# A recurrent attention layer and a two-layer block in one kernel: another written order, constants made on VectorE, and transposes of five late units given to the DMA crossbar

## The chip, the cores and the metric

The kernel runs on one core of one Trainium2 chip. The metric is the device time of one execution in microseconds (us); below it is better. The core has five engines with instruction queues of their own: TensorE (PE in the profile, its weight loads PEld), VectorE (DVE), ScalarE (ACT), GpSimd (POOL) and SyncE (SP), which here only issues DMAs. Every queue is in order: an instruction that waits holds up all behind it on its engine.

## The reference

First a recurrence with a decaying state runs over 768 time steps, for 4 batches and 8 heads of size 48. Its result is reshaped to 3072 tokens of 384 numbers, which pass through a block with a hidden layer of 1024, a softmax-like gate, a normalization and an output product.

```
# r, k, v, w: (4, 8, 768, 48), u: (8, 48)
for t in range(S):
    cur = outer(u * k[t], v[t])
    y[t] = r[t] @ (state + cur)
    state = w[t][:, None] * state + outer(k[t], v[t])
x = y as (3072, 384)
h = x @ w_in                                  # (3072, 1024)
solu = h * softmax(h)
ln = (solu - mean(solu)) / sqrt(var(solu) + 1e-6) * g_ln
out = ln @ w_out                              # (3072, 384), float32
```

## The kernel before

The work is cut into 24 units: six chunks of 128 time steps for each of four batches, chunk by chunk, batch by batch. Unit i works on batch i % 4 and chunk i // 4. So units i and i + 4 are tied by the state of their batch, and units 0 to 3 have no state before them.

A unit goes through these stages; the short names are the words of the written order. Loads: LW, LK, LR, LV bring w, k, r and v of the unit, 192 KB each in rows of 192 bytes. `lw` takes the logarithm of w on ScalarE, `cum` sums it over time with two matmuls against the triangular constants `uti_neg` and `uts`, `ex` takes the exponential in PSUM, and `kp` (DVE) multiplies it with k and r. `krk` and `krr` turn the two halves of the product on TensorE, four 128x128 blocks each, and `kr` copies the result from PSUM into `kr_s`. `M` multiplies the turned k with the turned r, head by head; `m` copies the scores, either with the triangular mask (DVE) or without it (ScalarE), in which case GpSimd masks them afterwards (`sel`). `p`, `q`, `dg` and `dv` make the bonus term with u; `vb` casts v to bf16. `Y` forms y from scores and state, `y` copies it. `S`, `et` and `st` carry the state on. `X` turns y on TensorE in three blocks, and `xT` copies them.

The second part: `H` is the hidden product (24 matmuls), `e` its exponential (ScalarE), `he` the gated value (DVE), `hq` its square. `Oa` and `Ob` are the output product in two halves of the hidden size; beside each output matmul of 385 columns stand two of one column, which sum for the normalization. `sq`, `qm` and `lv` make the scale per token, `o` scales, `out` stores.

One-time work: LI and LO load w_in and w_out (1.5 MB each), `wi` casts, `gw` multiplies w_out with the gain, `mn` takes a column mean with eight matmuls, `mc` copies it, `ce` subtracts it. LU, `us`, `uc` spread u; LG, `gs`, `gc` turn the gain. `hot` is a number of matmuls on zeros, of no use for the result.

Nothing schedules at run time. The order of all stages is written out as one text, `ORDER`, and every word is one call: a stage name, a unit number and, after a dot, an engine (a, d, p), a DMA queue (s for SP, a for ACT) or a PSUM slot. A wrapper, `InOrder`, keeps each engine's instructions in the order in which the calls were made. Because nearly all instructions are recorded inside that wrapper, the profile shows one line for them, L89, and they are told apart by the names of their tiles.

Rings of buffers bound how far one engine runs ahead: 7 for the loads of w, k, r and v, 10 for lw and vb, 6 for kp, kr and dv, 4 for most others. DMAs of SP and ACT share eight completion semaphores in turn, so a DMA also waits until the one eight places earlier has landed. All stores are issued by SP in this kernel.

Before the first word of the order, the constants are made: `warm`, the columns of ones and the zero paddings of `lw` and `kp` by memsets on DVE; the triangles, the identities, `halves`, `off_blocks` and `keep` by memsets and selects on GpSimd. The functions `turned_kr` (KD) and `turned_x` (XD) exist, but no word calls them:

```
    def turned_kr(i, x):
        sp.dma_start_transpose(out=kr_s[i % NKP], in_=kp_t[i % NKP].rearrange("t j h d -> t (j h d)"))

    def turned_x(i, x):
        sp.dma_start_transpose(out=xT_t[i % NWK], in_=y_t[i % NWK])
```

Of the kernel before, what the change touches and what calls it, by code (L numbers as in the profile page):

```python
# [8 lines left out]
F32 = mybir.dt.float32  # L9
BF16 = mybir.dt.bfloat16  # L10
# [11 lines left out]
LW0.a LK0.s LU0.a LR0.s LW1.a LW2.s hot4.s3 LG0.s LK1.s lw0 LV0.a cum0.b0 LR1.s us0.s0 ex0 hot2.s3 uc0 lw1 LV1.s  # L22
p0 kp0 LW3.a LK2.a LR2.s krk0.s3 q0 krr0 cum1.b1 kr0.a hot2.s2 LV2.s LK3.a M0.b0 LR3.s p1 gs0.s1 ex1 m0.d
hot3.s3 LI1.s lw2 q1 dg0 cum2.b0 lw3 hot2.s3 kp1 vb0.p LI0.a S0.s2 dv0 vb1.a dg1 hot1.s3 ex2 Y0.is0 et0 LV3.a
cum3.b1 LI2.s p2 kp2 krk1.s3 gc0 LO0.s ex3 st0 LW4.s krk2.s1 q2 krr1 LO1.s krr2 kp3 kr1.a hot3.s2 dv1 LK4.s
kr2.d y0.a p3 M1.b0 LK5.a S1.s2 dg2 krk3.s3 vb2.a m1.d krr3 et1 wi0.a S2.s0 wi1.p M2.b1 st1 X0.s1 kr3.a m2.d
Y1.is2 LR4.s wi2.p et2 y1.a M3.b0 xT0.d LV4.a X1.s3 q3 m3.d H0.b1 dv2 gw1.a dg3 gw2.d e0 Y2.is2 LW5.s xT1.d
gw3.p st2 H1.b0 y2.a he0 lw4 gw0.a X2.s1 LR5.s e1 gw7.d cum4.b1 gw4.d hot2.s3 gw6.d gw5.d ex4 he1 vb3.p mn0.s3
LW6.s LV5.a dv3 xT2.a LK6.s kp4 S3.s0 mc0 Y3.is2 LR6.s lw5 ce6.d krk4.s1 ce3.d hq0.a cum5.b0 ce4.d krr4 ce2.d
H2.b1 ce7.d ex5 LW7.s ce1.d ce5.d ce0.d y3.a LK7.s p4 kp5 et3 Oa0.s3 lw6 e2 LR7.s kr4.d p5 krk5.s2 cum6.b0 st3  # L30
hq1.a Ob0 vb4.p he2 LW8.s q4 krr5 ex6 S4.s1 LK8.s kr5.d sq0 M4.b1 lw7 Oa1.s0 kp6 et4 m4.a LR8.s X3.s2 qm0 st4
vb5.p M5.b0 xT3.a cum7.b1 dg4 sel4 lv0 krk6.s1 LV6.s Ob1 m5.d ex7 LW9.s dv4 lw8 S5.s2 kp7 o0.a krr6 LK9.s p6
cum8.b0 sq1 et5 Y4.ns3 kr6.d ex8 H3.b1 q5 LV7.s y4.d hq2.a kp8 q6 LR9.s krk7.s1 e3 X4.s3 st5 LW10.s vb6.p M6.b0
krr7 xT4.d Oa2.s2 dg5 m6.a LK10.s qm1 kr7.d dv5 krk8.s3 lv1 Ob2 he3 out0 sel6 o1.a lw9 M7.b0 out1 dg6 S6.s1 sq2
m7.a LV8.s hq3.d krr8 cum9.b1 LR10.s Y5.ns0 vb7.p qm2 kr8.d lv2 H4.b0 p7 LW11.s et6 y5.d ex9 st6 p8 lw10 kp9
LV9.s X5.s3 S7.s0 e4 Oa3.s1 q7 o2.d vb8.a he4 out2 cum10.b1 dv6 xT5.a krk9.s2 et7 LK11.s ex10 Y6.ns3 q8 krr9 st7
LV10.s H5.b0 hq4.a kp10 sel7 LR11.s kr9.a y6.d M8.b1 dg7 LW12.s S8.s0 lw11 m8.d Ob3 dv7 et8 e5 LV11.s vb9.p
krk10.s3 st8 X6.s2 LK12.s p9 M9.b1 he5 xT6.a Y7.ns0 sq3 m9.a krr10 LR12.s S9.s2 dg8 cum11.b0 et9 LW13.s y7.d
H6.b1 lw12 dv8 ex11 kr10.d LK13.s p10 qm3 lv3 kp11 Oa4.s0 LR13.s e6 q9 st9 X7.s3 cum12.b0 LW14.s xT7.a Ob4 he6
p11 ex12 LV12.s krk11.s2 sel9 sq4 Y8.ns3 o3.a kp12 H7.b1 hq5.a out3 vb10.p qm4 y8.d q10 LK14.s lv4 dg9 M10.b0 e7  # L40
Oa5.s1 LR14.s m10.d vb11.p q11 o4.a krr11 LW15.s X8.s3 lw13 dg10 Ob5 p12 xT8.a out4 he7 kr11.a S10.s0 dv9 S11.s3
LV13.s dg11 sq5 hq6.a Y9.ns2 vb12.p qm5 cum13.b0 y9.d dv10 LK15.s H8.b1 et10 ex13 st10 LR15.s et11 lw14 kp13
Oa6.s2 LW16.s e8 hq7.d krk12.s0 lw15 M11.b0 p13 st11 LK16.s Ob6 lv5 he8 o5.a q12 krr12 m11.a Y10.ns3 out5 kr12.d
krk13.s1 cum14.b1 LR16.s y10.d sq6 krr13 sel11 ex14 cum15.b0 LW17.s kr13.d Oa7.s0 ex15 qm6 LV14.s kp14 p14
Y11.ns3 lw16 X9.s1 Ob7 kp15 lv6 dv11 LK17.s vb13.a xT9.d p15 o6.a M12.b1 y11.d M13.b0 m12.a X10.s1 out6 m13.d
krk14.s2 q13 S12.s3 LR17.s hq8.a krr14 H9.b1 dg12 LV15.s vb14.p xT10.d sq7 q14 et12 qm7 st12 LW18.s lv7 krk15.s1
dg13 e9 X11.s3 sel12 H10.b0 o7.d kr14.a out7 he9 dv12 LK18.s Y12.ns0 xT11.a p16 krr15 LR18.s Oa8.s2 e10 y12.d
kr15.d q15 LV16.s cum16.b1 he10 S13.s0 ex16 dv13 Ob8 LV17.s et13 kp16 q16 X12.s3 LW19.s Y13.ns1 sq8 xT12.a st13
M14.b0 vb15.p M15.b1 LK19.s m14.a y13.d krk16.s3 S14.s0 hq9.d krr16 LR19.s m15.a S15.s1 p17 qm8 kr16.d H11.b0
LW20.s et14 dg14 lv8 sel14 st14 et15 LK20.s dg15 H12.b1 e11 vb16.p o8.d sel15 st15 out8 lw17 Oa9.s3 he11 LV18.s  # L50
e12 vb17.p dv14 S16.s0 LV19.s hq10.a he12 Ob9 dv15 LR20.s et16 cum17.b0 st16 q17 Y14.ns2 LV20.s ex17 X13.s1
y14.d M16.b1 sq9 Oa10.s0 lw18 kp17 LW21.s m16.a Y15.ns2 qm9 xT13.d LK21.s cum18.b0 hq11.d lv9 krk17.s1 lw19
H13.b1 LR21.s o9.d p18 vb18.a dg16 ex18 LV21.s y15.d dv16 krr17 e13 Ob10 kp18 LW22.s sel16 X14.s3 hq12.a kr17.d
S17.s2 LK22.s cum19.b0 q18 he13 Oa11.s1 xT14.a LR22.s ex19 p19 X15.s3 lw20 M17.b1 out9 xT15.d Ob11 sq10 kp19
vb20.p m17.a LW23.s q19 Y16.ns3 qm10 dg17 et17 vb19.a cum20.b0 p20 LV22.s y16.d lv10 H14.b1 dg18 sq11 ex20 sel17
LK23.s st17 lw21 o10.d LR23.s Oa12.s3 e14 kp20 dv17 krk18.s2 Ob12 out10 hq13.a p21 qm11 he14 krk19.s0 LV23.s
lv11 krr18 q20 cum21.b0 sq12 o11.d krr19 ex21 H15.b1 p22 qm12 kr18.d out11 lv12 kr19.d vb21.p Oa13.s1 dv18 kp21
e15 X16.s2 o12.d Y17.ns0 xT16.a M18.b0 hq14.a y17.d out12 krk20.s3 Ob13 he15 lw22 X17.s0 m18.a krk21.s2 xT17.d
krr20 cum22.b1 dg19 krr21 sq13 sel18 ex22 qm13 S18.s0 dg20 H16.b0 kr20.d hq15.a q21 kr21.d lv13 kp22 Oa14.s3
dv19 e16 dv20 M19.b1 et18 Y18.ns2 he16 m19.a Ob14 lw23 sel19 y18.d M20.b1 sq14 M21.b0 o13.d Oa15.s2 m21.a st18  # L60
out13 m20.d krk22.s1 X18.s0 cum23.b0 xT18.a krr22 Ob15 ex23 hq16.d vb22.p dg21 kr22.a Y19.ns0 q22 kp23 H17.b1
vb23.a dv21 qm14 sq15 y19.d lv14 Y20.ns1 e17 p23 o14.d H18.b0 dg22 out14 sel21 qm15 y20.d lv15 krk23.s0 he17 e18
Oa16.s3 dv22 krr23 o15.a he18 q23 Ob16 kr23.a out15 X19.s1 M22.b1 xT19.d M23.b0 hq17.d X20.s2 S19.s0 xT20.a
hq18.d Oa17.s1 m22.a dg23 Y21.ns2 et19 m23.a sel22 st19 H19.b1 sq16 sel23 qm16 y21.d lv16 Oa18.s0 e19 dv23
X21.s2 Ob17 he19 H20.b0 sq17 o16.d xT21.d out16 Y22.ns3 qm17 e20 Y23.ns2 y22.d Ob18 y23.d hq19.a he20 H21.b1
lv17 o17.d X22.s3 Oa19.s2 e21 out17 xT22.d hq20.d X23.s1 sq18 H22.b0 he21 xT23.d Ob19 qm18 hq21.d e22 H23.b1
sq19 lv18 qm19 he22 Oa20.s3 e23 o18.d hq22.d Oa21.s1 out18 lv19 he23 Ob20 o19.d Ob21 sq20 hq23.d out19 Oa22.s0
sq21 qm20 qm21 lv20 Oa23.s2 lv21 o20.d o21.d out20 Ob22 out21 Ob23 sq22 qm22 lv22 sq23 qm23 o22.d lv23 out22
o23.a out23
# [27 lines left out]
def kernel(  # L97
# [14 lines left out]
    C = 128  # L112
# [20 lines left out]
    def bank(shape, dtype, slot, name):  # L133
# [15 lines left out]
    dve.memset(warm, 0.0)  # L149
    uti_neg = consts.tile([C, C], BF16)  # L150
    pool.memset(uti_neg, -1.0)
    pool.affine_select(out=uti_neg, in_=uti_neg, compare_op=ALU.is_ge, fill=0.0, base=0,
                       pattern=[[1, C]], channel_multiplier=-1)
    uts = consts.tile([C, C], BF16)
    pool.memset(uts, 1.0)
    pool.affine_select(out=uts, in_=uts, compare_op=ALU.is_gt, fill=0.0, base=0,
                       pattern=[[1, C]], channel_multiplier=-1)
    ident_f = consts.tile([C, C], F32)
    pool.memset(ident_f, 0.0)
    pool.affine_select(out=ident_f, in_=ident_f, compare_op=ALU.not_equal, fill=1.0, base=0,  # L160
                       pattern=[[-1, C]], channel_multiplier=1)
    ident = consts.tile([C, C], BF16)
    pool.tensor_copy(out=ident, in_=ident_f)

    halves = consts.tile([C, C], BF16)
    pool.memset(halves, 0.0)
    pool.memset(halves[0:2, :], 1.0)
    pool.affine_select(out=halves[0:2, :], in_=halves[0:2, :], compare_op=ALU.is_ge, fill=0.0, base=0,
                       pattern=[[1, C]], channel_multiplier=-64)
    pool.affine_select(out=halves[0:2, :], in_=halves[0:2, :], compare_op=ALU.is_gt, fill=0.0, base=64,  # L170
                       pattern=[[-1, C]], channel_multiplier=64)
    off_blocks = consts.tile([C, HP, 2], BF16)
    pool.memset(off_blocks, 0.0)
    pool.memset(off_blocks[0:2], -30000.0)
    pool.affine_select(out=off_blocks[0:2], in_=off_blocks[0:2], compare_op=ALU.not_equal, fill=0.0, base=0,
                       pattern=[[0, HP], [-1, 2]], channel_multiplier=1)

    one_col = consts.tile([C, 2], BF16)
    dve.memset(one_col, 1.0)
    inv_col = consts.tile([C, 1], BF16)  # L180
    dve.memset(inv_col, 1.0 / RDF)
    ones_row = consts.tile([1, C], F32)
    dve.memset(ones_row, 1.0)

    lw_t = ring("lw", NLW, [C, H, 64], BF16)
    kp_t = ring("kp", NKP, [C, 2, H, 64], BF16)
# [369 lines left out]
```

The softmax here doesn't subtract the row's maximum and nothing guards it: scores larger than these inputs give would overflow.

## Time and profile before

| what | us |
|---|---|
| median of 5 runs | 154.59 |
| lowest and highest run | 152.16 and 155.85 |
| profiled execution, its own time | 154.59 |
| span of that execution in the profile | 152.8 |
| PE busy | 137.3 |
| DVE busy | 127.8 |
| ACT busy | 117.8 |
| POOL busy | 95.3 |

The span runs from the first to the last instruction; the time of an execution also holds what lies around it. Busy time of PE is modelled with pipelined matmuls, so it tells that TensorE had work, not that it ran at its peak; the pace is better read from the distance of the starts. The page cuts the span into 40 slices and gives each engine one digit for each, in tenths. The chain goes back from the last instruction, at each step to what released it or to the instruction before it on its engine. A line with SPq or ACTq is a DMA issue on that queue, and its length is the time of the issue.

### The profile page before, as it was taken

What the parts mean: (1) busy time and instruction counts of PE and PEld (TensorE: products, weight loads), DVE (VectorE), ACT (ScalarE), POOL (GpSimd) and SP (SyncE); (2) the same over time, 40 slices, a digit from 0 to 9 for tenths busy, and PEclk for the clock granted to TensorE, in tenths of its full rate; (3) what the DMA queues carried; (4) which work ended last, traced back from release to release, by engine and by line L of the source; (5) the groups of instructions that cost most, each with busy time, mean ns of one, the idle gap of its engine ahead of it and who ended that gap; (6) DMA issues with size and microseconds to landing.
All of it is one profiled execution on the core that took longest, in us unless ns stands there. A gap on an engine that the chain in (4) does not pass through costs nothing.

```text
span 152.8 us, 5260 instructions
## 1 busy us (share of the span) xinstructions
PE 137.3 (90%) x2158; PEld 106.8 (70%) x2158; DVE 127.8 (84%) x235; ACT 117.8 (77%) x238; POOL 95.3 (62%) x127
## 2 busy tenths in 40 slices
PE   4799786879999998999993999999999999999980
PEld 1145565467788876887793797878887888889750
DVE  5209797989999997999983999999998998688941
ACT  3464857499999997999895588999898998475442
POOL 7484993621979769992928999299937691500000
PEclk9999999999999999999999999999999999999999
DMA  5999999899994999989999999999930111011142
GB/s 107 259 259 334 399 328 267 174 205 188 226 197 124 232 186 205 202 196 206 236 203 205 192 191 222 186 212 220 229 114 4 51 56 51 4 51 56 51 158 103
DMA packets 104825, 27.08 MB, mean 177 GB/s; under 512 B 100313, under 2 KB 104418, under 8 KB 104802
## 3 DMA queue, kind: packets, MB, share of 16 engines
q1 hardware_dynamic: 94256, 24.26, 69.4%
q10 hardware_dynamic: 10546, 2.49, 7.2%
q8 instruction: 17, 0.28, 0.7%
q14 instruction: 6, 0.05, 0.1%
HBM read 22.03 MB, written 4.72 MB: 175 GB/s over the span
## 4 chain that ended last, share of the span: by engine, by line
PE 48%; DMA 12%; SPq 11%; DVE 10%; POOL 9%; issue 4%; ACT 3%; ACTq 0%; DVEq 0%; POOLq 0%
PE o_ps L89 21%; PE h_ps L89 12%; SPq L89 11%; DMA w_in<-in_w_dram 8%; DMA kr_in<-in_r_dram 3%; PE kr_ps L89 3%; PE y_ps L89 3%; PE cum_ps L89 3%; POOL p L89 3%; POOL q L89 2%; PE m_ps L89 2%; PE s_ps L89 2%; POOL m L89 2%; DVE kp L89 2%; DVE st L89 2%
## 5 line engine op out<-in xcount | busy, mean ns | idle before, releaser
L89 PE MATMUL o_ps<-w,he 128*128 128x385 bf16 x192 | 45.8, 325 | 0.1
L89 PE MATMUL h_ps<-xT,win_sb 128*128 128x128 bf16 x576 | 35.9, 219 | 0.3 <-DVE xT L89 0.3
L89 PEld LDWEIGHTS <-win_sb 128*128 128x128 bf16 x576 | 33.0, 98 | 0.9 <-issue 0.4
L89 PE MATMUL o_ps<-inv_col,e 128*128 128x1 bf16 x192 | 31.8, 166 | 0.0
L89 PE MATMUL o_ps<-one_col,hq 128*128 128x1 bf16 x192 | 31.4, 164 | 0.0
L89 DVE TENSOR_TENSOR he<-h_ps,e 128x1024 bf16<-128x1024 f32 x24 | 29.1, 1216 | 2.6 <-ACT e L89 2.5
L89 ACT ACTIVATE e<-h_ps 128x1024 bf16<-128x1024 f32 x24 | 24.5, 1020 | 4.7 <-PE h_ps L89 4.6
L89 DVE TENSOR_TENSOR kp<-cum_ps,kr_in 128x768 bf16<-128x768 f32 x24 | 22.7, 949 | 5.7 <-ACT cum_ps L89 5.5
L89 PEld LDWEIGHTS <-hq 128*128 128x128 bf16 x192 | 18.5, 96 | 12.7
L89 POOL TENSOR_TENSOR p<-kr_in 128x384 bf16<-128x384 f32 x24 | 24.7, 1029 | 3.5 <-DMA kr_in<-in_r_dram 3.5
L89 POOL TENSOR_TENSOR dv<-vb,dg 128x384 bf16<-128x384 bf16 x24 | 19.8, 829 | 9.4 <-DVE dg L89 7.3
L89 POOL TENSOR_SCALAR_AFFINE_SELECT m<-m 128x1024 bf16<-128x1024 bf16 x15 | 16.8, 1121 | 12.7 <-ACT sq L89 5.6
L89 POOL TENSOR_TENSOR q<-p,u_bc 128x384 bf16<-128x384 bf16 x24 | 21.8, 910 | 1.9 <-DMA kr_in<-in_k_dram 1.7
L89 ACT ACTIVATE cum_ps<-cum_ps 128x768 f32<-128x768 f32 x24 | 19.2, 802 | 4.7 <-PE cum_ps L89 4.6
L89 PEld LDWEIGHTS <-kp 128*128 128x128 bf16 x272 | 17.5, 98 | 5.8 <-DVE kp L89 2.1
L89 PE MATMUL kr_ps<-ident,kp 128*128 128x128 bf16 x192 | 18.0, 223 | 2.2 <-ACT xT L89 0.9
L89 PEld LDWEIGHTS <-he 128*128 128x128 bf16 x192 | 18.4, 96 | 0.9
L89 PEld LDWEIGHTS <-e 128*128 128x128 bf16 x192 | 18.5, 96 | 0.3
L89 ACT CAST m<-m_ps 128x1024 bf16<-128x1024 f32 x15 | 15.1, 1016 | 0.7 <-PE m_ps L89 0.6
L89 ACT ACTIVATE lw<-w_in 128x384 bf16<-128x384 f32 x24 | 12.4, 523 | 3.7 <-DMA w_in<-in_w_dram 3.7
L89 DVE TENSOR_TENSOR m<-m_ps,keep 128x1024 bf16<-128x1024 f32 x9 | 10.9, 1215 | 4.2 <-PE m_ps L89 4.2
L89 ACT ACTIVATE hq<-he 128x1024 bf16<-128x1024 bf16 x13 | 13.8, 1058 | 0.0
(82 smaller groups left out, 263.0 us busy)
## 6 DMA issues: line engine op xcount, KB each, us to landing
kr_in<-in_r_dram SPq DMA_DIRECT2D x24, 192.0 KB, 4.0
out_dram<-o SPq DMA_DIRECT2D x24, 192.0 KB, 2.9
kr_in<-in_k_dram SPq DMA_DIRECT2D x21, 192.0 KB, 3.7
w_in<-in_w_dram SPq DMA_DIRECT2D x21, 192.0 KB, 3.9
v_in<-in_v_dram SPq DMA_DIRECT2D x20, 192.0 KB, 4.0
wout_f<-in_moe_w_out_dram SPq DMA_DIRECT2D x2, 768.0 KB, 7.7
win_f<-in_moe_w_in_dram SPq DMA_DIRECT2D x2, 512.0 KB, 5.0
v_in<-in_v_dram ACTq DMA_DIRECT2D x4, 192.0 KB, 4.5
```

The lines of the kernel that those rows point to most:

```text
L89: made = make(*args, **kwargs)
```

## The change

The order text is replaced by another. In it:

- `turned_kr` (KD) takes the place of `krk`, `krr` and `kr` for units 19 to 23, and `turned_x` (XD) the place of `X` and `xT` for the same units. Both are DMA transposes on SP's queue, from SBUF to SBUF.
- Eight stores (units 5, 6, 11, 13, 17, 18, 22, 23) and the load of the gain are issued by GpSimd instead of SP. ScalarE issues 9 DMAs instead of 12.
- The bonus is added by DVE in the copy of y for all units but one (20 units before), so one identity matmul in `Y` instead of four.
- `m` with the mask on DVE 12 times instead of 9, `sel` 12 instead of 15; `o` on ScalarE 17 times instead of 8; `hq` on ScalarE 15 instead of 13; two of eight `ce` on GpSimd; 25 warm-up matmuls instead of 19.
- The loads of a unit stand later in the text against the matmuls in the last third; the loads of units 0 to 4, but v of unit 4, stand ahead of w_in and w_out.

Outside the order: the constants become a stage (`pc`) that the order calls; their memsets are on DVE, four selects stay on GpSimd. `halves` and `off_blocks` use rows 0 and 32 instead of 0 and 1 and need no select. `keep` is the same tile as `uts`. u is rounded to bf16 (`ur`) before the matmul that spreads it. Stages that treat a unit in halves are added (hidden, exponential, gate, square, output columns, sums, store); no word of the new order calls them, and the last unit goes through the same stages as the others.

The diff, cut to its core:

```
-LW0.a LK0.s LU0.a LR0.s LW1.a LW2.s hot4.s3 LG0.s LK1.s lw0 LV0.a cum0.b0 LR1.s us0.s0 ex0 hot2.s3 uc0 lw1 LV1.s
...
-sq21 qm20 qm21 lv20 Oa23.s2 lv21 o20.d o21.d out20 Ob22 out21 Ob23 sq22 qm22 lv22 sq23 qm23 o22.d lv23 out22
-o23.a out23
+LG0.p pc0 LW0.s LR0.a LK0.s LR1.a hot6.s3 LU0.s LW1.s LW2.s LV0.s lw0 cum0.b0 LW3.s ur0 hot1.s3 ex0 us0.s0
...
+ex1 krr0 hot6.s2 uc0 LK2.a LW4.s lw2 p1 kp1 kr0.a cum2.b0
...
+Y3.ns3 H1.b1 gw3.d e0 st3 y3.d gw0.a LW6.s gw6.d X3.s0 gw7.d gw4.a gw5.d LK6.s e1 he0 mn0.s2 LR6.s vb4.p lw5 he1
+dv4 xT3.a cum5.b0 mc0 LW7.s S4.s1 ex5 Y4.ns3 ce5.d ce2.d H2.b1 hq0.a ce0.p kp5 vb5.a ce7.d H3.b0 LK7.s ce3.d et4
...
+sq10 ex20 Y16.ns3 out9 qm10 xT15.d H14.b1 sq11 lv10 kp20 KD19 vb19.a o10.a y16.d S16.s1 e14 hq13.d H15.b0 out10
...
+ex23 sel20 qm14 st18 sq15 lv14 kp23 q22 Y19.ns1 o14.a Y20.ns3 y19.d e17 KD23 H18.b0 p23 y20.d he17 q23 Oa16.s0
+out14 e18 XD19 dv21 qm15 S19.s1 lv15 he18 Ob16 hq17.a LV23.s M22.b1 XD20 dg22 o15.a M23.b0 Oa17.s3 m22.d sq16
...
+out16 he19 XD22 Oa18.s0 e20 st19 H21.b1 hq19.a qm17 dg23 he20 dv23 Y23.ns2 e21 Ob18 y23.d lv17 XD23 Oa19.s1 he21
...
+Ob22 o21.a Ob23 out21 sq22 qm22 lv22 sq23 qm23 o22.d lv23 o23.a out22.p out23.p

-    pool.memset(uti_neg, -1.0)
-    pool.affine_select(out=uti_neg, ...)
...
+    keep = uts
+
+    def constants(i, x):
+        dve.memset(warm, 0.0)
+        dve.memset(uti_neg, -1.0)
+        dve.memset(uts, 1.0)
+        dve.memset(ident, 0.0)
+        dve.memset(ident_f, 0.0)
+        pool.affine_select(out=uti_neg, ...)
+        pool.affine_select(out=uts, ...)
+        pool.affine_select(out=ident, ...)
+        pool.affine_select(out=ident_f, ...)
+        ...
+        for row, own in ((0, 0), (32, 1)):
+            dve.memset(halves[row:row + 1, 64 * own:64 * own + 64], 1.0)
+            dve.memset(off_blocks[row:row + 1, :, 1 - own], -30000.0)
...
-    ones_row = consts.tile([1, C], F32)
+    ones_row = consts.tile([1, C], BF16)
...
-    queue = {"s": sp, "a": act}
+    queue = {"s": sp, "a": act, "p": pool}
...
+    def round_u(i, x):
+        dve.tensor_copy(out=u_b, in_=u_row)
...
-    pe.matmul(ps["u"], lhsT=ones_row, rhs=u_row, start=True, stop=True)
+    pe.matmul(ps["u"], lhsT=ones_row, rhs=u_b, start=True, stop=True)
...
-        sp.dma_start(out=out[b * S + c * C:b * S + (c + 1) * C, :], in_=o_t[i % NWK])
+        queue[x or "s"].dma_start(out=out[b * S + c * C:b * S + (c + 1) * C, cols], in_=o_t[i % NWK][:, cols])
```

## The prediction

> **What bounds the kernel now.** I read the page first: the 40 slices, then the chain.
>
> ```profile
> span 152.8 us, 5260 instructions
> PE   4799786879999998999993999999999999999980
> DMA  5999999899994999989999999999930111011142
> GB/s 107 259 259 334 399 328 267 174 205 188 226 197 124 232 186 205 202 196 206 236 203 205 192 191 222 186 212 220 229 114 4 51 56 51 4 51 56 51 158 103
> PE 48%; DMA 12%; SPq 11%; DVE 10%; POOL 9%; issue 4%; ACT 3%; ACTq 0%; DVEq 0%; POOLq 0%
> ```
>
> A slice is 3.82 us. TensorE has holes in the first eight slices and is full afterwards; the DMA engines are full up to slice 30 (some 112 us) and nearly empty later. So the start hangs on transfers and the short queues, the rest on TensorE, with the loads close behind it. The chain in order of time shows where that changes:
>
> ```profile
> 26.11 3.90 DMA w_in<-in_w_dram
> 30.02 0.44 ACTq L89
> 30.50 0.13 ACT xT L89
> ...
> 30.88 0.48 ACT mean_sb L89
> 31.36 0.43 ACT lw L89
> 31.84 0.49 PE cum_ps L89 x2
> ...
> 32.55 1.34 PE h_ps L89 x24
> 33.89 0.87 PE o_ps L89 x12
> ...
> 38.16 0.19 PE x_ps L89 x3
> ...
> 53.85 4.16 DMA w_in<-in_w_dram
> ...
> 141.58 5.98 PE o_ps L89 x84
> ```
>
> The columns are start, length, what. From 31.84 us (cum5 in the written order) the chain is mostly TensorE. Its pieces, these and further ones of the same list, price a stage by its pace: H 1.34, Oa and Ob 0.83 each, krk and krr (four transposes) 0.235 each, X 0.18, cum 0.33, M 0.33, Y 0.38, S 0.46 us. Summed along the written order, 122.1 us of useful TensorE work stand in the whole kernel and 110.1 us from cum5 on. The last matmul ends at 148.40. The busy times by stretch give the holes after 32 us:
>
> ```profile
> 80.00:90.00 10.00, 7.66 (x145) 6.39 (x143) 7.22 (x11) 6.21 (x13) 9.12 (x11) 1.00 0.97 200
> 130.00:140.00 10.00, 10.00 (x176) 8.70 (x174) 8.32 (x16) 5.76 (x13) 2.10 (x3) 1.00 0.12 43
> ```
>
> (stretch, length, busy PE, PEld, DVE, ACT, POOL, clock, DMA share, GB/s). All stretches together leave 3.64 us of holes, 2.34 of them in 80 to 90. So 148.40 - 31.84 - 3.64 = 112.9 us for 110.1 us of prices: one priced us is 1.026 real ones. After the last matmul stand 4.4 us of scaling and store. The profiled execution took 154.59 us, 1.79 beyond its span, and is the median of the five runs (152.16 to 155.85); I sum against it.
>
> **What the Trainium skill says.** "VectorE: DVE Perf Modes", The three transpose paths: a 128x128 bf16 block takes TensorE 390 ns and the DMA crossbar 1309 ns. This trace has TensorE's at 223 ns, pipelined to 59 ns (0.235/4); it has no crossbar transfer. "DMA: Bandwidth & Descriptors", Latency and other measured facts: crossbar transposes move 261 GB/s. Same page, Issuing engines are not separate DMA queues: all queues share the 16 engines; so the new ones queue behind loads. Same page, SWDGE vs HWDGE vs iDMA: descriptors of a GpSimd DMA are written by software; first byte about 1 us against 0.6. The trace has no such DMA.
>
> **The change part by part.**
>
> *TensorE work.* Units 19 to 23 lose krk, krr (2 x 0.235 each) and X (0.18): 5 x 0.65 = 3.25 us. Only one unit instead of four adds its bonus by an identity matmul (0.16 us apart by the starts of the matmuls around it): 0.48. Together 3.73 priced, 3.8 us real, all on a full engine. The six additional warm-up matmuls lie in the first waits. The stages for a unit in halves are defined, but no word of the order calls them: nothing.
>
> *The start.* Constants leave GpSimd (its selects and memsets end at 4.82 us), but lw0 also ends at 4.82, so that alone gives nothing. The u matmul in bf16 takes some 0.3 instead of 1.64 us; krk0 stood behind it and two warm-ups until 8.36. What sets the start is ScalarE. It issued 12 loads and stood behind their semaphores: 2.4 us before gw, 2.1 before xT, 1.4 before gr, 1.3 before vb in the table of waits. Now it issues nine. From lw0 (4.30) to mc0 the new order gives it 6 lw at 0.52, 5 ex at 0.80, 5 kr at 1.01, 4 et at 0.18, 4 xT at 0.48, 2 e at 1.02, 2 vb at 0.51, 3 gw at 0.62, uc, gc, wi0, y2 and mc0 (2.66 together) and seven issues at 0.38: 25.1 us. With the first two waits of before (0.89 + 0.78) mc0 ends at 31.1; before it ended at 31.36. By then TensorE has done mn0, cum5 and S4: 105.3 priced us are left, at 31.84 some 104.6, against 110.1. That is 5.5 x 1.026 = 5.6 us, 3.8 of it the missing work: the start gives 1.8 us. Bounds: the weights stand five loads later in the queue, which can take it all (0); 3 if ScalarE finds no wait.
>
> *The loads in the middle.* SP's issues show the pace:
>
> ```profile
> 29.28 0.70 SPq L89 DMA_DIRECT2D w_in<-in_w_dram  x1
> 33.49 1.36 SPq L89 DMA_DIRECT2D w_in<-in_w_dram  x1
> 41.77 0.74 SPq L89 DMA_DIRECT2D w_in<-in_w_dram  x1
> 89.61 0.61 SPq L89 DMA_DIRECT2D w_in<-in_w_dram  x1
> 108.70 41.64 SPq L89 DMA_DIRECT2D out_dram<-o  x13
> ```
>
> These are w of units 7, 8, 10, 20, then stores alone. From 33.49 to 41.77 lie 8 transfers (1.03 us each), from w12 (53.85) to w20 36 (0.99 each), with the DMA share near 1. The new order wants w7 to w12 in 17.2 priced us (17.7 real) with 19 transfers, 0.93 each, and w12 to w20 in 35.6 us with 38, 0.94 each. At the old pace the loads fall behind by 1.9 and another 1.9 us, and a load leads its use by only some 4 us, about what it needs to land (3.7 to 4.0). So holes come back: I take 3.3 us against 3.64, bounds 0 and 7. Gain 0.3.
>
> *The crossbar.* KD moves 256 KB, XD 96. Stores land 2.9 us after issue with 192 KB, so at 261 GB/s KD needs about 3.2 us, XD 2.5 (estimate, from below). From above, eight and three blocks at 1309 ns in sequence: 10.5 and 3.9. Leads in TensorE work from KD to M: 5.7, 9.1, 7.2, 7.5, 3.9 us for units 19 to 23; from XD to H 4.1, 4.2, 4.0, 4.3, 3.1. I take 5 and 3.5, since loads share the rings: KD23 is then 1.1 late, XD23 0.4: a loss of 1.5, bounds 0 and 40. On SP, behind a waiting KD or XD, stand LK23, LR23, LV23 and stores; the loads come late in the new order anyway (LR23 at 29.7 priced us before the end instead of 42.8) but only kp23 and vb23 wait for them, 5 us on.
>
> *The engines beside.* Copies saved and shifted: DVE loses some 6 us of 127.8 (nine scalings of o at 0.61, three kr at 0.68, seven xT at 0.35, against three m at 1.22 and three y at 0.55, the rest small), ScalarE gains 2 of 117.8, GpSimd about 3 of 95.3 (nine DMAs estimated at 1 us, less constants and three selects). None becomes longer than TensorE, so nothing. If that cover fails, a store on GpSimd that waits for its o holds up dv or sel behind it, at most 1 us each, six times in the middle: in the range.
>
> *The end.* The order of the last stages is as before; out22 and out23 go from SP to GpSimd. Its first byte is 0.4 us later by the skill, and out23 stands behind out22's descriptors: 0.7 lost, bounds 0 and 1.5.
>
> Sum: -3.8 - 1.8 - 0.3 + 1.5 + 0.7 = -3.7; 154.59 - 3.7 = 150.9 us.
>
> **Rivals.**
>
> *Slow crossbar (slower).* The ten transposes go through one queue. From KD19 to M23 lie 40.0 - 19.8 priced us = 20.7 us for five KDs. The other terms bring 5.2 us; these are gone when five KDs take 25.9, 5.2 us each, and the kernel is slower by 2% from 5.8 each. At 7 us, between my ends, 35 - 20.7 - 5.2 = +9: 164 us. At 10.5 each, XD behind, H23 begins beyond 175: about 190. For it: the block price in the skill. Against: the engines are nearly empty after 112 us, and 261 GB/s.
>
> *The loads take it back.* All 3.8 us of lag come on top of the 3.3 and the start gives nothing: 150.9 + 1.8 + 2.5 = 155.2. For it: DMA share 0.97 to 1.04 from 50 to 110. Against: slices 2 and 3 moved 259 GB/s, so 205 need not be the limit.
>
> *The new order fits.* No holes (-3.3), no late transpose (-1.5): 146.1. Against: every order written out meets waits it did not count on; this one left 3.64.
>
> *It does not do what it says*: then the kr and X matmuls would still be in units 19 to 23; the change plainly leaves them out, so no chance is set aside.
>
> **How the numbers follow.** Forecast 0.56 (147 to 154; 0.38 below 151.5, 0.18 above), slow crossbar 0.20, loads 0.15, fit 0.09. Two per cent of 154.59 is 3.1 us, about what a measurement tells from no change. Faster: 0.38 + 0.09 = 0.47; same 0.18 + 0.15 = 0.33; slower 0.20. The range 146 to 160 leaves out most of the slow crossbar (0.16) and a little of the fit (0.04).
>
> **What would show it.** Right: mc0 near 31 us with unit 4's scores already done; Oa0 at 35 to 36; TensorE full to 143; holes of 3 to 4 us around lw9 to lw13; DMA shares of 0.3 and more after 110 us; M23's wait about 1 us; last store landing 3.5 us after o23. Wrong: mc0 beyond 33.5; KD landing over 5.8 us; waits of M or H for DMA above 5 us in total; TensorE holes above 7 us before 110.

## The result, and the profile after

The changed kernel takes 154.3 us (median of 43 runs), the kernel before 153.35 (80 runs). Medians are over all runs; the ratios in this document compare only the runs of each kernel that lie within about 1.5% of its fastest: 1.0052 here, interval 1.003 to 1.0073. Measured again later, the ratio came out at 0.999 (0.9936 to 1.0043). The changed kernel is no faster and at most 0.7% slower; 150.9 us was forecast. The execution of before that the forecast summed against, 154.59 us, was 1.2 us above the usual median.

The profiled execution of the changed kernel took 153.39 us. Its page:

```profile
span 151.5 us, 5192 instructions
PE   6599887787999999989999859999999999999960
PEclk9999999999999999999999968999999999999998
DMA  5999999999899899999999999099899965412042
GB/s 100 252 249 257 297 397 353 228 178 212 174 204 184 206 210 261 184 196 258 195 241 181 175 212 206 5 202 212 154 219 216 167 173 114 143 30 87 35 156 104
PE 25%; POOL 15%; DMA 15%; issue 13%; SPq 11%; ACT 11%; DVE 7%; POOLq 0%; ACTq 0%; DVEq 0%
```

A slice is 3.79 us. TensorE is full late in the kernel, as before, but slices 22 and 23 (83 to 91 us) show 8 and 5, and in slices 23 and 24 the granted clock dips to 6 and 8 tenths. The share of TensorE in the chain that ended last fell from 48% to 25%; GpSimd's rose from 9% to 15%. The busy times by stretch say the same (stretch, length, PE, PEld, DVE, ACT, POOL, clock, DMA share, GB/s):

```profile
80.00:90.00 10.00, 7.37 (x124) 5.99 (x122) 9.19 (x12) 8.43 (x15) 7.62 (x9) 0.93 0.90 183
90.00:100.00 10.00, 9.92 (x149) 7.50 (x148) 8.79 (x15) 7.28 (x16) 7.34 (x9) 0.90 0.59 127
130.00:140.00 10.00, 10.00 (x176) 8.74 (x173) 9.04 (x16) 7.41 (x13) 1.95 (x3) 1.00 0.24 69
```

In 80 to 90 us VectorE is busy for 9.19 us with only 12 instructions, in the next 10 us for 8.79 us with 15: one of the 12 is long. The chain in order of time (start, length, what) and the timeline of VectorE and GpSimd there:

```profile
83.24 0.56 DVE y L87
83.80 3.83 DVE hq L87
87.62 0.48 issue
88.10 0.55 DVE st L87
88.65 0.04 issue
88.69 1.63 PE o_ps L87 x12
```

```profile
83.71 4.46 DVE L87 TENSOR_TENSOR hq<-he 128x1024 bf16<-128x1024 bf16 x1
83.47 0.99 POOL L87 TENSOR_TENSOR p<-kr_in 128x384 bf16<-128x384 f32 x1
84.42 0.49 POOL L87 CAST vb<-v_in 128x384 bf16<-128x384 f32 x1
84.88 1.08 POOL L87 TENSOR_SCALAR_AFFINE_SELECT m<-m 128x1024 bf16<-128x1024 bf16 x1
85.94 0.82 POOL L87 TENSOR_TENSOR dv<-vb,dg 128x384 bf16<-128x384 bf16 x1
86.72 0.90 POOL L87 TENSOR_TENSOR q<-p,u_bc 128x384 bf16<-128x384 bf16 x1
```

The square of unit 8 (`hq8.d`) takes 4.46 us; the other eight on VectorE take 0.68. It ends at 88.17, 0.55 us after GpSimd's row of five ends. Behind it stand st, xT and he on VectorE, and behind st TensorE (the second line gives stretch, length, busy PE, clock, DMA share, GB/s):

```profile
88.69 0.48 PE L87 MATMUL o_ps<-w,he 128*128 128x385 bf16 x1 [2.27 <-DVE st L87]
90.00:91.00 1.00, 1.00 (x14) 0.50 1.11 235
```

The wait is not all. Behind it the granted clock is 0.50 until about 92 us, and a matmul of 385 columns takes 0.48 us, where 0.33 is usual. That the wait brings the lower clock was not tested.

To compare stages of kernels whose order differs, I use the measure of the forecast: to the start of unit i's hidden product H I add the priced TensorE work that follows, times 1.026. The sum is the time at which the last matmul would end if no hole came any more. Work that an order leaves out counts as gained from the start, at its price. "Before again" is another execution of the kernel before (see below).

| at | shown before | before again | changed |
|---|---|---|---|
| H0 | 140.3 | 140.4 | 136.4 |
| H2 | 144.8 | 144.8 | 139.2 |
| H9 | 146.2 | 146.2 | 142.1 |
| H11 | 148.7 | 146.6 | 142.4 |
| H12 | 148.7 | 146.6 | 146.2 |
| H23 | 148.3 | 146.6 | 146.1 |
| last matmul | 148.40 | 146.69 | 146.27 |
| span less that | 4.4 | 4.35 | 5.2 |

Against before again, the changed kernel is 5.6 us ahead at H2 (3.8 of it is the work left out), still 4.2 at H11, and 0.4 at H12. Of the 3.8 us lost from H11 to H12, 2.4 are the wait and 1.3 the slower matmuls behind it. From 93 us on it loses nothing: the work from H12 to the last matmul, priced 51.9 us, takes 53.35, and about 53.3 are due at the pace of 1.026. The store at the end adds 0.8 us to the tail. So the gain is made, and most of it is spent in one place.

### The profile page after: what moved, and what is told of

Read it like the earlier page. It is cut to its first block, busy times and chain, and to the rows that moved or that the text cites. A ratio compares the mean times of both kernels' runs of the same rounds, so it can differ in the third digit from the quotient of the medians.

```text
span 151.5 us, 5192 instructions
## 1 busy us (share of the span) xinstructions
PE 134.8 (89%) x2105; PEld 104.3 (69%) x2105; DVE 128.9 (85%) x229; ACT 119.0 (79%) x243; POOL 95.8 (63%) x123
## 4 chain that ended last, share of the span: by engine, by line
PE 25%; POOL 15%; DMA 15%; issue 13%; SPq 11%; ACT 11%; DVE 7%; POOLq 0%; ACTq 0%; DVEq 0%
SPq L87 11%; PE o_ps L87 10%; PE h_ps L87 7%; DMA wout_f<-in_moe_w_out_dram 6%; DMA kr_in<-in_r_dram 6%; POOL p L87 4%; POOL q L87 3%; POOL m L87 3%; DVE hq L87 3%; ACT e L87 3%; POOL dv L87 3%; DMA v_in<-in_v_dram 2%; PE s_ps L87 2%; PE y_ps L87 2%; ACT hq L87 2%
## 5 line engine op out<-in xcount | busy, mean ns | idle before, releaser
L87 PE MATMUL o_ps<-w,he 128*128 128x385 bf16 x192 | 46.3, 331 | 2.7 <-DVE st L87 2.7
L87 POOL TENSOR_TENSOR p<-kr_in 128x384 bf16<-128x384 f32 x24 | 24.1, 1008 | 9.2 <-DMA kr_in<-in_k_dram 5.5
L87 POOL TENSOR_TENSOR dv<-vb,dg 128x384 bf16<-128x384 bf16 x24 | 20.3, 850 | 10.4 <-DVE dg L87 10.2
L87 PEld LDWEIGHTS <-kp 128*128 128x128 bf16 x232 | 15.1, 99 | 2.9 <-issue 0.5
L87 ACT ACTIVATE hq<-he 128x1024 bf16<-128x1024 bf16 x15 | 15.8, 1055 | 0.8 <-DVE he L87 0.8
L87 POOL TENSOR_SCALAR_AFFINE_SELECT m<-m 128x1024 bf16<-128x1024 bf16 x12 | 13.3, 1112 | 4.9 <-ACT m L87 4.8
L87 POOL CAST vb<-v_in 128x384 bf16<-128x384 f32 x18 | 9.0, 502 | 10.7 <-DMA v_in<-in_v_dram 10.7
L87 DVE TENSOR_TENSOR m<-m_ps,uts 128x1024 bf16<-128x1024 f32 x12 | 14.5, 1218 | 0.3 <-PE m_ps L87 0.2
L87 PE MATMUL kr_ps<-ident,kp 128*128 128x128 bf16 x152 | 14.6, 224 | 0.0
```

The lines of the kernel that those rows point to most:

```text
L87: made = make(*args, **kwargs)
```

## The experiments

All times and ratios are against the kernel before on the same chip. Edits are words of the written order.

### The same again, and the parts one by one

The changed kernel once more, unedited:

> The changed kernel once more, for a second profile and the spread. Theory (GpSimd starves VectorE): somewhere between 60 and 110 us one squaring hq on VectorE, two SBUF operands, lasts several times its 0.68 us while GpSimd runs without a pause, TensorE stands for over 1 us and loses over 2 us there; 154 +- 1 us. Rival (the loads): TensorE's holes come from landings, hq never over 1.5 us. Rival (chance of one execution): no hole of more than 1 us in the middle in this profile.

153.41 us, ratio 0.999 (0.9936 to 1.0043). The square of unit 8 took 3.60 us. The projected end went from 143.2 (H11) to 144.8 (H12): the event comes in both profiled executions of this kernel, but cost 1.6 us here against 3.8, and less than the 2 us expected. The wait is shorter here, and behind it the clock stays at 1.00 and the matmuls are not slower:

```profile
88.59 0.32 PE L86 MATMUL o_ps<-w,he 128*128 128x385 bf16 x1 [1.41 <-DVE st L86]
```

Units 19 to 23 turned on TensorE again:

```
- KD19 ... XD19            (and 20 to 23)
+ krk19.s1 krr19 kr19.d ... X19.s3 xT19.a
```

> Undoes one part: units 19 to 23 are turned on TensorE again (krk, krr, kr and X, xT in place of KD and XD), the order else kept. If the crossbar gives what its TensorE work is worth and costs no stall (3.25 us of matmuls, 3.3 at the pace of the chip): 3 to 3.5 us slower than the changed kernel, the rest of TensorE's progress alike up to 100 us. If the transposes in flight cost as much as they save: equal within 1 us. If they hurt: faster.

160.97 us, ratio 1.0518 (1.0444 to 1.0593): twice the loss that was expected. The projected end is 3.4 us later at H2 (142.6), which is the price of the work put back; the square was 4.63 us long and cost 4.0 us (H11 to H12), again with a clock of 0.50 behind the wait; from H16 on 5 us more were lost, 3.7 of them in waits for kr and xT, so my places for these stages are worse than the DMAs'. It shows what the transposes' work costs in this order, not what an order made for TensorE transposes would take.

The square of unit 8 on ScalarE:

```
- hq8.d
+ hq8.a
```

> One instruction moved: the square of unit 8, which lasted 4.46 us on VectorE in the profile of the changed kernel, goes to ScalarE (1.05 us). Starvation theory: the hole at 86 to 88 us and the drop of TensorE's clock after it go, 2 to 3.5 us faster than the changed kernel, unless another hq takes its place. Rival, the hole comes from loads or from GpSimd's own lateness: the hole stays, equal within 1 us, or 1 us slower since ScalarE is busy there.

151.39 us, ratio 0.9891 (0.9853 to 0.993). No long square, clock 1.00 until the matmuls end, 0.5 us lost between H11 and H12. One word is worth 1.0% against the second measurement of the changed kernel (0.999) and 1.6% against the first (1.0052).

All stores on SP:

```
- out5.p out6.p out11.p out13.p out17.p out18.p out22.p out23.p
+ out5 out6 out11 out13 out17 out18 out22 out23
```

> All stores back on SP's queue, as in the kernel before. If GpSimd's stores cost only at the end: 0.5 to 1 us faster (the last store lands 2.8 us after its scaling instead of 3.6). If GpSimd's six stores in the middle (0.6 us each) also held up masks and bonus terms: 1 to 3 us faster. If the stores on SP hold up loads and transposes behind them: slower by 1 us or more.

151.05 us, ratio 0.9867 (0.9803 to 0.9931). Tail 4.35 us. I had not counted on what the timeline showed:

```profile
86.28 1.55 DVE L85 TENSOR_TENSOR hq<-he 128x1024 bf16<-128x1024 bf16 x1
86.21 1.09 POOL L85 TENSOR_SCALAR_AFFINE_SELECT m<-m 128x1024 bf16<-128x1024 bf16 x1
87.27 1.26 POOL L85 TENSOR_TENSOR dv<-vb,dg 128x384 bf16<-128x384 bf16 x1
```

The square is still on VectorE and beside the same row, but waits only for the select and then goes ahead of dv, which is 0.4 us longer for it. So the stores on GpSimd have to do with the long square.

Only the last two stores on SP, and both remedies at once:

```
c_tail:  out22.p out23.p -> out22 out23
c_both:  all eight stores as above, and hq8.d -> hq8.a
```

> The changed kernel with only the last two stores (out22 and out23) back on SP; the six stores in the middle stay on GpSimd. Theory: only the tail changes, from 5.2 to about 4.35 us, so 0.8 us are gained: 152.5 to 153 us, ratio to the kernel before 0.994 to 0.998, and the square of unit 8 is still 3.5 to 4.6 us long. Rival (the stores at the end make up most of what the stores on SP gave): 151.1 us, ratio 0.987. If the ratio is near 1.0, the tail isn't worth what the profiles show.

153.42 us, ratio 0.9989 (0.9953 to 1.0024), square 4.04 us. The tail fell to 4.74, not to 4.35, and the time stands where the changed kernel's own (0.999) does. No gain from the end stands clear of the noise; most of what the stores on SP gave (0.9867) came from the six in the middle.

> The changed kernel with two edits at once: every store is issued on SP again, and the square of unit 8 goes to ScalarE. Alone the first took 2.0% off the kernel before's ratio-to-1 time and the second 1.1%. Theory (both remove the same event, a VectorE square held up by a row of GpSimd instructions; the stores at the end on SP save a further 0.8 us of tail): the two don't add, since both remove the same 3 to 4 us; from the 151.05 of the stores alone a few tenths go, 150.3 to 151.0 us, ratio 0.980 to 0.986, last matmul about 145.3, tail 4.35 us. Rival (the two take away different losses): they add, some 149.4 us, ratio 0.975 or less, last matmul near 144.

149.99 us, ratio 0.9813 (0.9762 to 0.9864). This version beats both kernels, the one before by 1.9%. Its last matmul ends at 144.77, the tail is 4.36. The interval does not tell whether the two remedies add (0.976) or overlap (0.985). Its stretch of 80 to 90 us is full:

```profile
80.00:90.00 10.00, 10.00 (x177) 8.40 (x176) 7.45 (x14) 9.59 (x19) 8.83 (x12) 1.00 0.97 200
```

### What the base was worth, and the transposes in the old order

The kernel before, unedited:

> The kernel before once more, to see which of its holes come back in another execution: the hole of 2.3 us at 81 to 83 us, where the scores of a unit were late because GpSimd waited for a transfer of v. Theory (it is an accident of the shown execution): the last matmul ends near 146 to 147 us instead of 148.40, with a span of some 151. Rival (the hole belongs to the kernel): 148 us and the hole at the same place.

Its span is 151.0 us, its last matmul ends at 146.69, and the hole of 2.3 us at 81 to 83 us is 0.2. The two timelines show why (what stands in brackets is the idle time before and what ended it); the first line is of the shown execution, the second of this one:

```profile
80.88 0.50 POOL L89 CAST vb<-v_in 128x384 bf16<-128x384 f32 x1 [3.66 <-DMA v_in<-in_v_dram]
```

```profile
78.74 0.50 POOL L89 CAST vb<-v_in 128x384 bf16<-128x384 f32 x1 [1.60 <-DMA v_in<-in_v_dram]
```

The load of v came 2 us later in the shown execution than here. The forecast took its 3.64 us of holes for the kernel's own; as far as two executions can tell, 2 of them were this accident.

The old order with only the transposes given to the DMA:

```
- krk19.s0 krr19 kr19.d ... X19.s1 xT19.d    (and 20 to 23)
+ kp19 KD19 ... y19.d XD19
```

> The kernel before, in its own order, with only the turning by DMA added: in units 19 to 23 the two groups of transposes of k and r on TensorE with their copy, and the three of y with theirs, are left out; one DMA for k and r stands directly behind the product that makes them, one for y directly behind y. Theory (TensorE's work is the path, and a transpose of some 5 us by DMA fits in its lead): 3.25 us of priced work by 1.026 are gone, so 150.0 us, ratio 0.978. Bounds: a loss when the transposes by DMA wait behind loads that stand ahead of them on SP, 153 to 156 us. Rival (in this order TensorE's end hangs on the loads up to unit 23 and on the engines beside): 152.5 to 153.5 us, ratio near 1, with as much more waiting of TensorE as there is less work.

153.41 us, ratio 1.0032 (1.0 to 1.0064): the rival came true. At H2 the projected end is 3.2 us ahead of before again (141.6), at H14 2.8 us (144.4), at H22 nothing is left (147.1). The stretches where it goes, and two of TensorE's waits (line, what it waited for: total, times, longest):

```profile
110.00:120.00 10.00, 8.96 (x148) 6.70 (x147) 8.45 (x15) 8.70 (x17) 6.14 (x8) 1.00 0.93 198
120.00:130.00 10.00, 9.65 (x180) 8.22 (x176) 8.09 (x15) 7.33 (x16) 7.51 (x8) 1.00 0.38 96
130.00:140.00 10.00, 9.36 (x165) 8.23 (x164) 7.72 (x13) 5.30 (x12) 0.00 (x0) 1.00 0.22 62
```

```profile
PE h_ps L85 <- DMA xT<-y: 0.6, 1, 0.6
PE m_ps L85 <- DMA kr<-kp: 0.6, 1, 0.6
```

2.03 us of holes stand in 110 to 140 us, where before again had none; 1.2 of them are waits for transposes; two waits of 0.4 us for VectorE's he are listed besides. So less TensorE work was no gain in an order that isn't made for it. In the changed order no wait of TensorE for these transposes is listed.

### What holds the square up

The first theory was that VectorE can't get in while GpSimd runs back to back.

```
phase: products | selects | casts  x 7 to 14 on GpSimd
       tensor_mul(hq, he, he)      x 4 on VectorE, issued first
```

> A measurement of one question; the whole computation is left out, zeros are stored. Six phases, each after a wait: four VectorE squares of 128x1024 (bf16) alone; four of them beside eight GpSimd products of two tiles (128x384, bf16) back to back; beside seven GpSimd selects of 128x1024; beside fourteen GpSimd casts of 128x384; six VectorE products of a PSUM tile with an SBUF tile beside eight GpSimd products; six VectorE sums over the free axis beside eight GpSimd products. Theory (a VectorE operation with two SBUF inputs can't start or go on while GpSimd runs without a pause): 0.68 us alone, the first square beside products or selects ends only when GpSimd's row ends, 4 to 8 us; the products with PSUM and the sums keep their 0.55 us. Rival (the two engines take turns, instruction by instruction): each square is 1.2 to 2 us long beside GpSimd. Second rival (no interference; the long square of unit 8 had another cause, such as a late semaphore): 0.68 us in all phases.

Squares alone took 0.68 to 0.69 us. In each row the first two squares were through before GpSimd had begun in earnest; the other two took 1.3 us beside products, 1.6 beside selects, 1.0 beside casts. Products with PSUM and sums kept 0.54 to 0.55. That is turns, not a lock-out. But VectorE had been there first. With GpSimd ahead:

```
phase: row = (f32 product, cast, select, product, product) x 3 on GpSimd
       VectorE: 4 products with PSUM, then 5 x (square, 2 products with PSUM)
```

> A measurement of one question; the whole computation is left out, zeros are stored. In the measurement before, VectorE's squares were first at the memory and each took 1.0 to 1.2 us beside GpSimd. Here GpSimd's row starts first, and VectorE comes some 2 us later, with five squares of 128x1024 that each stand between products with PSUM. Eight phases: the row that stood beside the long square in the changed kernel (product of two f32 tiles, cast, select, two bf16 products, back to back, three times), the same with one more product of VectorE ahead, fourteen bf16 products, thirteen f32 products, twelve selects, the row with squares of half the size, the row with copies instead of squares, and squares alone. Theory (the engine that comes second waits until the other pauses): one square takes 3 us or more in the rows, until the row ends. Rival (turns, instruction by instruction): no square takes over 1.8 us in any phase, and then the 4.46 us of the changed kernel have a cause that isn't in the row of GpSimd alone. Second rival (it is one kind of instruction, most likely the f32 product or the cast): the long squares stand in one of the pure phases only.

The longest of twenty-five full-size squares beside GpSimd took 1.32 us. Beside bf16 products, for instance:

```profile
36.29 1.22 DVE L35 TENSOR_TENSOR hq<-he 128x1024 bf16<-128x1024 bf16 x1
38.49 1.16 DVE L35 TENSOR_TENSOR hq<-he 128x1024 bf16<-128x1024 bf16 x1
```

Then with the tiles of the kernel itself, and with a store ahead of the row in half the phases:

```
- q <- src_b, src_b; m <- mat
+ p <- kr_in[:, 0, :, :48], kr_in[:, 1, :, :48]; m <- m; dv <- vb, dg broadcast
+ phases 13 to 24: pool.dma_start(out, zero) ahead of the row
```

> A measurement of one question; the whole computation is left out, zeros are stored. GpSimd runs the row that stood beside the long square, now with the kernel's own shapes (the f32 inputs as 48 of every 64 elements, the select in place, the factor broadcast), ten instructions back to back; VectorE comes with one square of 128x1024 after two to seven products with PSUM, in steps of half a product, so that it comes in every kind of instruction of the row. Twelve phases without and twelve with a store issued on GpSimd ahead of the row. Theory A (whoever comes while the f32 product or the cast runs, waits out the row): the phases in which the square comes there take 3 us or more, with and without the store. Theory B (a store issued by GpSimd shortly before sets it): long squares in the second twelve phases only. Rival (turns in every case): no square over 1.8 us, and what holds the square in the kernel is not in these instructions alone.

At most 1.50 us in all twenty-four phases, with and without the store, wherever the square came. In this measurement the theory of the moment (A) falls, and the row isn't the cause by itself. With a store, though, the square came 1.7 to 4.9 us after it was issued; in the kernel 8 to 10 us lie between. So four variants of the kernel, with the TensorE transposes put back (a_peturn, where the square is long too), one profiled execution each:

```
p_stores56:  out5.p -> out5, out6.p -> out6
p_early8:    hq8.d y13.d ...
p_next8:     y13.d ... st14 hq8.d ...
p_late8:     y13.d ... st14 ... xT13.d hq8.d ...
```

> The changed kernel with units 19 to 23 turned on TensorE again (the variant that took 160.97 us, whose square of unit 8 was 4.63 us long), and with the stores of units 5 and 6, the last two that GpSimd issues before that square, on SP. Theory B (GpSimd's stores shortly before cause the long square): at most 1.6 us. Theory A (the moment at which VectorE comes decides): 3.5 to 4.7 us again where it comes within the f32 product or the cast, else short.

> The same variant, stores as they were, with the square of unit 8 ahead of the sum y of unit 13 on VectorE, some 0.5 us earlier, at GpSimd's bf16 product. Theory A: 1.0 to 1.6 us. Theory B, or a row that keeps VectorE out from any point: 4 to 5.5 us.

> The same variant with the square of unit 8 one instruction later, behind st of unit 14, some 0.5 us later, at the end of the f32 product or in the cast. Theory A: 3 to 4 us, as long as what is left of the row. Rival (only one moment is bad, by chance): 1.0 to 1.6 us.

> The same variant with the square of unit 8 two instructions later, behind the copy of xT of unit 13, at GpSimd's select or product dv. Theory A: 0.7 to 1.6 us. Theory B, or a row that keeps VectorE out from any point: what is left of the row, up to 2.5 us.

The square's line in each, in this order:

```profile
84.45 1.64 DVE L86 TENSOR_TENSOR hq<-he 128x1024 bf16<-128x1024 bf16 x1
```

```profile
84.33 4.66 DVE L86 TENSOR_TENSOR hq<-he 128x1024 bf16<-128x1024 bf16 x1
```

```profile
85.42 3.17 DVE L86 TENSOR_TENSOR hq<-he 128x1024 bf16<-128x1024 bf16 x1
```

```profile
87.91 2.90 DVE L86 TENSOR_TENSOR hq<-he 128x1024 bf16<-128x1024 bf16 x1
```

The last three come at the f32 product, the select and the select, and all three last until GpSimd's row ends, 0.5 to 0.6 us beyond it. Without the stores of units 5 and 6 on GpSimd, issued at 70 and 76 us, the square takes its turn after the select (1.64 us, 0.04 above the expected bound), and 0.3 us are lost from H11 to H12 against 4.0 with these stores. What that is worth in time isn't shown: the one execution took 159.49 us, and six runs with these stores 159.29 to 165.1 (the other three variants 164.5, 160.6 and 162.57). Theory A is refuted in the kernel as well, since a square that comes at the select is long with the stores (3.17 and 2.90 us) and short without; theory B holds there, in a_spout and p_stores56. The early square came at the f32 product, not at the bf16 product that I had counted on, so it doesn't test that place.

In all seven executions with the long square (six kernels) GpSimd had not stood idle from its store at 75 to 78 us to the end of the row; in the five that took turns (1.41, 1.41, 1.42, 1.55 and 1.64 us in before, before again, b_turn, a_spout and p_stores56; in the first three it is the square of another unit) no store was in the row. And in the changed kernel run again, where GpSimd had stood idle between its next stores and a later square (113.4 us), that square took 1.41. So I measured a row that runs on from a store:

```
phases 5 to 8:   copy; pool.dma_start(out, zero); row x 3
phases 9 to 12:  copy; pool.dma_start(out, zero); copy that waits for VectorE; row x 3
```

> A measurement of one question; the whole computation is left out, zeros are stored. GpSimd runs a row of fifteen instructions of the kernel's shapes, and VectorE comes with one square after four to nine products with PSUM. Four phases without a store, four with a store that GpSimd issues straight ahead of the row, four with a store after which GpSimd waits for VectorE before its row begins. In the seven kernels that showed a square of 2.9 to 4.7 us, GpSimd had not been idle from its last store on to the end of the row; in the six that showed 1.4 to 1.6 us at this place there was no store in the row. Theory C (a row that runs on from a store keeps VectorE out until GpSimd pauses): in the second four phases the square takes what is left of the row, 3 to 12 us, in the first and the last four at most 1.5. Rival (the store matters in the kernel only, with something that this measurement does not have): at most 1.5 us in all twelve.

At most 1.47 us in all twelve phases. The rival holds as far as this reaches: in the four phases whose row runs on from the store, the square came 2.0 to 4.9 us after the store was issued. The kernel's 8 to 10 us were reached only in the phases where GpSimd had paused, so a delayed effect of the store in an unbroken row is not ruled out. What belongs to the long square stays open. The runs show that taking these two stores off GpSimd ends it, that taking the square off VectorE ends it, and that neither the moment nor the instructions of the row bring it about by themselves.

## Why the forecast was wrong

*The engines beside (nothing): the step that failed.* The forecast said that none becomes longer than TensorE, so that they cost nothing, and named for a failing cover a store on GpSimd that holds up dv or sel, at most 1 us each. What failed is that a sum of busy times can't show a loss that lies between two engines: one square stood up to 3.8 us behind GpSimd, and TensorE behind it. That cost 1.6 to 4.0 us from H11 to H12 by execution (the changed kernel 3.8, again 1.6, c_tail 2.1, with units turned on TensorE 4.0); taken away by one word it was worth 1.0 to 1.6%. The mechanism that I named, a store waiting for its o, is not what was seen. Nor was VectorE's sum right: its busy time was to fall by 6 us and rose by 1.1, to 128.9, with 3.8 us of waiting in the square and some 2.2 in the additions below among them.

Between H2 and H4 the same two engines meet a second time, which no experiment here was made for. VectorE adds the column mean (`ce`). In before GpSimd is idle beside it, and eight of these take 2.31 us. In the changed kernel GpSimd runs two `ce` of its own and then `p`; three of VectorE's six take 1.07 to 1.16 us each, the other three 0.34 to 0.36. The first line is of before, the others of the changed kernel:

```profile
31.40 2.31 DVE L89 TENSOR_TENSOR w<-w,mean_sb 128x384 bf16<-128x384 bf16 x8 [0.62 <-ACT mean_sb L89]
33.23 2.42 DVE L87 TENSOR_TENSOR w<-w,mean_sb 128x384 bf16<-128x384 bf16 x3
33.09 2.07 POOL L87 TENSOR_TENSOR p<-kr_in 128x384 bf16<-128x384 f32 x2
33.36 1.50 PE L87 MATMUL h_ps<-xT,win_sb 128*128 128x128 bf16 x24 [0.34 <-DVE kp L87]
36.17 0.34 PE L87 MATMUL x_ps<-ident,y 128*128 128x128 bf16 x3 [0.41 <-DVE y L87]
36.90 0.34 PE L87 MATMUL o_ps<-w,he 128*128 128x385 bf16 x1 [0.39 <-DVE st L87]
```

TensorE waits there for kp, y and st, which stand between these additions on VectorE, and 2.0 us are lost from H2 to H4 (139.2 to 141.2; 139.7 to 141.6 in the second execution; 0.1 in before again). That the lengthened additions are what loses them is read from the order of the instructions, not tested by an edit.

The Trainium skill bears on both places: "SBUF — State Buffer", Who interferes with whom, says that a VectorE instruction with two SBUF inputs contends with a GpSimd instruction that reads SBUF, because the two share a pair of ports, and calls this an exclusive lock. The measurements agree: the square took 0.68 us alone and 0.7 to 1.6 beside GpSimd, while products with one PSUM input kept their 0.55. As I read the page, the wait is for one instruction of the other engine, some 1 us here; a wait over up to five instructions is seen in seven executions and in no measurement of the parts.

*The base.* The sum started from 154.59; the usual execution takes 153.35. That it was the median of five runs, with 152.16 among them, was bad luck; taking the holes of one execution as the kernel's own was the mistake. It does not explain the miss. The high start alone put the forecast 1.2 us too high; the holes made the loads term 1.8 us too kind (3.64 against the 1.8 that before again loses after H2). The two nearly cancel.

*TensorE work and start (-3.8 and -1.8): right.* 5.6 us ahead were forecast at 32 us; 5.6 were measured at H2, 5.1 in the second execution. `mc0` ends at 31.06 (31.1 forecast):

```profile
30.56 0.50 ACT L87 CAST mean_sb<-mean_ps 128x384 bf16<-128x384 f32 x1
```

*Loads in the middle (3.3 us of holes): right in size, partly by luck.* From H2 to H11 3.2 us were lost in the shown execution; 3.5 in the second one. But the forecast saw the holes around lw9 to lw13, and 2.0 of these us (1.9) were gone before H4, at VectorE's additions; Oa0 began at 36.90 us, where 35 to 36 were expected. From H4 to H11 only 1.2 us were lost (1.6), behind lw and kp that waited for w and r (0.97 and 0.73 us). Late loads did come, and cost less than the sum said.

*The crossbar (+1.5): no cost in this order.* The leads that the forecast counted, 3.1 to 9.1 us, were enough; its 5 us for k and r and 3.5 for y were close or high (issues: tile, queue, kind, count, median us to landing), and no wait of TensorE names a DMA:

```profile
kr<-kp SPq DMA_TRANSPOSE x5, 4.8
xT<-y SPq DMA_TRANSPOSE x5, 2.5
```

The slow rival (5.2 us each and more in one queue) did not come. The 261 GB/s of the forecast stand in the Trainium skill's "DMA: Bandwidth & Descriptors", Latency and other measured facts, for one kernel whose middle dimension is not contiguous; for the contiguous case the page has some 350 to 400, so they were no bound from below. The skill's "VectorE: DVE Perf Modes", The three transpose paths, gives 1309 ns a block; eight in sequence would be 10.5 us (an estimate from that page), and 4.8 with the wait for other transfers included were measured. The measurement decides: the blocks of one transfer aren't paid one by one.

*The rivals.* "The loads take it back" came nearest in size (155.2; its own words, all 3.8 us of lag on top and no gain at the start, give 156.5), but for another reason: its start that gives nothing and its lag did not come. "The new order fits" (146.1) fails by the holes. That the change does not do what it says was never in question: units 19 to 23 have no transposes on TensorE.

*The end (+0.7):* 5.2 against 4.35 us in the profile, +0.8, though giving these two stores back to SP did not show in the time. The two stores have one line on GpSimd:

```profile
147.49 1.19 POOL L87 DMA_DIRECT2D out_dram<-o  x2 [8.10 <-DVE o L87]
```

Summed again against the usual execution: 5.6 gained by H2; 3.2 + 3.8 lost from there to H12, against 1.8 to the same place in before; 0.8 at the end. That is -5.6 + 5.2 + 0.8 = +0.4 us, the difference of the spans (151.46 and 151.04). Of the 7.0 us lost, 2.0 and 3.8 (1.3 of these at the lower clock behind the wait) fall in the two places where VectorE stands behind GpSimd, a term that the forecast put at nothing. With all stores on SP and the one square on ScalarE (c_both) the ratio is 0.981; the forecast amounted to 0.976.

## What to carry to other kernels

Before a step is priced against one profiled execution, ask which of its holes are waits for a transfer that another execution would not have; where the runs spread by 2%, a hole of 2 us at one late load is suspect. When a change gives GpSimd more work or stores, look at each VectorE instruction with two SBUF inputs beside it: it can be made to wait for GpSimd, though no semaphore says so, and giving one such instruction to ScalarE brought 1% by itself. Work taken off the bounding engine is a gain only in an order that has the lead for what replaces it: the same ten transposes gave nothing in the old order and met no wait in the new one.

## What the runs showed of the hardware

- A VectorE square of 0.68 us took 2.9 to 4.7 us in seven executions, to 0.5 to 0.6 us beyond the end of GpSimd's row, where GpSimd had issued a store 8 to 10 us earlier and not paused since; without that store 1.4 to 1.64. Not reproduced outside the kernel, where the square came at most 4.9 us after such a store.
- VectorE and GpSimd take turns otherwise: the one that comes second waits for one instruction of the other. A square of 0.68 us took up to 1.6 (m_port, m_row); an addition of two 128x384 tiles took 0.35 us alone and 1.07 to 1.16 behind a GpSimd instruction.
- Behind waits of TensorE of 2.27, 2.43 and 3.18 us near 89 us (changed kernel, a_peturn, p_early8) the granted clock was 0.50 for 3.1 to 3.4 us; behind waits of 1.41 to 1.85 us at that place (again, p_late8, c_tail) it stayed at 1.00. It isn't a rule: in before a wait of 2.32 us at 83 us was followed by 1.00.
- A DMA transpose of 256 KB landed 4.8 us after issue (3.6 in the old order), one of 96 KB 2.5, and held SP's queue for 1.2 to 3.2 us at issue. A plain load took SP mostly 0.4 to 1.2.
- A store of 192 KB landed 2.5 us after issue from GpSimd as from SP; its issue took GpSimd 0.54 to 0.64 us.
